# Inner form of one more fifth product, v asked for a unit sooner, and ScalarE's copies ahead of its sines, in a pooled-attention and snake-MLP kernel

## The chip, the cores and the metric

The kernel runs on one core of a Trainium2 chip. The metric is the device time of one execution in microseconds. The kernel before took 899.54 us (median of three runs, 898.81 to 899.56).

The engines are TensorE (PE; its weight loads are a row of their own, PEld), VectorE (DVE), ScalarE (ACT), GpSimd (POOL) and SyncE (SP), whose queue issues nearly all transfers here. Each engine runs its own instructions in program order and waits at an instruction whose inputs or whose place aren't ready.

## The reference

Everything is float32.

```python
def _attn_ref(q, k, v):              # each (8, 8, 576, 64)
    k_p = k.reshape(B, H, 72, 8, D).mean(axis=3)
    v_p = v.reshape(B, H, 72, 8, D).mean(axis=3)
    scores = np.matmul(q, k_p.transpose(0, 1, 3, 2)) / np.sqrt(D)
    attn = softmax(scores)           # over the 72 pooled keys
    return np.matmul(attn, v_p)

def _moe_ref(x, w_in, w_out, alpha): # x: (4608, 512), d_ff 2048
    h = x @ w_in
    s = np.sin(alpha * h)
    g = h + s * s / (alpha + 1e-09)
    return g @ w_out
```

The output of the attention, with heads side by side, is x.

## The kernel before, in words

**Stages.** The tokens go through the first matrix product in nine units of 512 tokens (units 0 to 8). While unit u is in TensorE, the attention of batch u+1 is worked out between its products. Units 1 to 6 are alike and last about 55 us each; the code calls them busy. Units 7 and 8 have no attention beside them. The second matrix product, `outputs`, fills the time from about 513 us on. The hidden values g go to DRAM (`g_bridge`) and come back.

**Seven products in place of eight.** Both matrix products are done by a scheme in which a 2x2 block product takes seven block products and some sums (`sums_of_x`, `combine_w_in`). In a unit there are four groups J = 0 to 3, each with seven slots k = 0 to 6. Slot number 7J + k is what the plan counts in, so group 1 has slots 7 to 13. In the slots the products come in the order 1, 5, 6, 2, 7, 3, 4. Each is four 128x128 by 128x256 matrix products, which the trace shows as eight records (an f32 product leaves two).

**Inner form.** `inner_product` works out one of these seven products by the same scheme once more, with blocks of 128 columns: seven small matrix products (fourteen records) in place of the eight records. It has four steps. Step a makes two of the small products in bank 7, and ScalarE copies them (L1062 into both halves of the result's bank, L1064 into a small tile m). Step b adds two products and ScalarE copies one quarter (L1068). Step d adds one product, and VectorE adds m (L1073). Step e adds the last two. The sums of weights come from `inner_w_in` once in unit 0, those of x from `inner_x` in slot 2 of each unit, both on GpSimd (L823). In busy units product 5 is done so in groups 2 and 3, and product 1 in group 3.

**Banks and the order within a group.** A group has four PSUM banks, b1, b6, b5, b7, drawn in turn from five, so b6, b5 and b7 of a group are b1, b6 and b5 of the group before, and its b1 is that group's spare, the b7 of the group before the last. Product 1 goes to b1; ScalarE copies it to b6 (L839), on which product 6 is added; b6 is copied to b7 (slot 3), and product 5's bank to an SBUF tile p5. Product 2 is added on b1, 7 on b7, 3 on b6 and 4 on b7. VectorE forms b7 + p5 in slot 5 and b6 + p5 in slot 6 (L838). Product 4 overwrites b7 after the first of these sums. ScalarE takes the sines (L1028) and squares (L1035); the last sines of a group are taken while the next group is in TensorE (`last_sines`, `squares`), and `finish` adds the squares on VectorE (L1080) before `store_g` sends the group off (L1094).

**Attention beside it.** `carry` writes the plan by hand: `at(slot, f)` puts a piece into a slot, where it is emitted at `extras()`. For units 1 to 6 it has the scores in slots 3 and 5 (L318) with their shifts on VectorE (L341, L342), then for four blocks i the exponentials on ScalarE (`exp`, L367), the reduction, reciprocal and scaling (`norm`, L373, L374 on VectorE, L375 on GpSimd) and the turning by VectorE (`turn`, L504 to L514). `move` sends the turned blocks to the tile aM, and `all_values` in slot 25 multiplies with v. Sines and exponentials have different tables on ScalarE: each change is an instruction of its own, ACT_TABLE_LOAD.

**v.** `load_v` issues six transfers (L141, L146) and has GpSimd add up the eight rows of each pool at once (`pool_rows`, L132). The smaller rest is added by `pool_v` in slot 12.

The plan for units 1 to 6, so far as the change touches it, is this:

```python
                at((8, 9, 10, 10)[i], A.exp, i)
                at((9, 10, 11, 12)[i], A.norm, i)
                at((12, 13, 13, 13)[i], A.turn, i)
            at(14, A.move, range(4))
            at(6, self.load_v, b)
            at(12, lambda: self.pool_v())
```

Of the kernel before, what the change touches and what calls it, by code (L numbers as in the profile page):

```python
# [19 lines left out]
P = 128  # L20
POOL = 8
TH = 256
JW = 2
# [17 lines left out]
class Kernel:  # L41
# [92 lines left out]
    def load_v(self, b):  # L134
# [12 lines left out]

        self.pool_rows(t, vm[:])

# [685 lines left out]
    def hidden(self, u, extra):  # L835
# [5 lines left out]
        busy = 0 < u < self.B - 1  # L841
        I5, I1 = ((2, 3), (3,)) if busy else {7: ((2, 3), (2, 3)), 8: ((2, 3), (2, 3))}.get(u, ((), ()))
        split = lambda J: u == 0 and J == 2
        end = lambda J: u == 0 and J == 3

# [31 lines left out]
        for slot in range(7 * self.NJ):  # L877
# [9 lines left out]
            if k == 0:  # L887
# [16 lines left out]
            elif k == 1:  # L904
                if not G.i1:
                    copy(G.b6[:], G.b1[:])
                if G.i5 and not G.i1:
                    self.last_sines(Q, 0)
# [8 lines left out]
            elif k == 2:  # L917
                if Q and not G.i5 and not split(J):
                    self.finish(Q)
                if not G.i1:  # L920
                    extras()
                if G.i1:
                    product(G, 6, G.b6, part=(0, 1))
# [15 lines left out]
            elif k == 3:  # L939
                late = J == 0 and busy  # L940
                if Q and not late and not G.i5 and not split(J):
                    self.store_g(Q)
# [10 lines left out]
                else:  # L953
                    copy(G.b7[:], G.b6[:])
                    if G.i5:
                        squares(Q, 1)
                        G.i5.d()
                        self.finish(Q)
                        self.store_g(Q)
                    else:  # L960
                        copy(G.p5[:], G.b5[:])
# [3 lines left out]
                    extras()  # L965
                    product(G, 2, G.b1)
            elif k == 4:
# [3 lines left out]
                else:  # L971
                    sin(G, 0, 0, G.b1)
                if not G.i5:
                    square(G, 0, 0)
# [4 lines left out]
                product(G, 7, G.b7, part=(0, 1))  # L979
                if G.i5:  # L980
                    if not G.i1:
# [41 lines left out]

    def sin(self, G, i, j, src):

        for jj in range(JW):
            f = i * self.K2 // 2 + G.J * JW + jj
            self.nc.scalar.activation(out=G.s[:, i, jj, j, :], in_=src[:, jj], func=AF.Sin, scale=self.al[:, f:f + 1])  # L1028
# [173 lines left out]
    def carry(self, u):  # L1202
# [6 lines left out]
        if u == 0:  # L1209
# [16 lines left out]
            at(7, self.load_v, 1)  # L1226
            at(7, lambda: self.pool_v())
            for i in range(2):
# [20 lines left out]
            at(9, self.load_q, 2)  # L1249
            at(23, lambda: self.inner_w_in(((5, 2, 4), (1, 3, 4)), (lambda w: [w[:, i * 2 * P:i * 2 * P + 2 * P] for i in range(8)])(self.q_tile(0))))  # L1250
            for e in range(2):
# [7 lines left out]
        if 0 < u < last:  # L1259
# [453 lines left out]
```

## Time and profile before

| | |
|---|---|
| median of three timed runs | 899.54 us |
| profiled execution, first to last instruction | 896.2 us |
| TensorE busy | 890.8 us, 99% |
| VectorE busy | 682.9 us, 76% |
| ScalarE busy | 438.6 us, 49% |
| GpSimd busy | 249.2 us, 28% |
| granted TensorE clock | 1.000 |
| length of a busy unit | 55.1 us (slot 25 at 129.9, 184.9, 240.0, 295.2 us) |

The page gives no other time of the profiled execution than its span; the timed runs include what lies around it. A line of the timeline gives the start, how long the instruction or the run of like instructions took, engine, line of the code, operation, the tiles written and read with their shapes, how many, and in brackets the idle time before it and what ended that. A line of the waits gives who waited for whom, the total in us, how often, and the longest. Records of TensorE overlap: the distance of two starts is the price of an instruction, and the length that is written is more than that. ScalarE's and VectorE's instructions overlap by about 0.1 us in the same way.

### The profile page before, as it was taken

The page shows a single profiled execution, that of the slowest core. Times are in us where ns is not written, and L with a number is a line of the kernel's source. Part 1 is how long each engine was busy: PE and PEld are TensorE (multiplying, and loading weights), DVE is VectorE, ACT ScalarE, POOL GpSimd, SP SyncE. Part 2 cuts the span into 40 slices and gives each one's busy share as a digit, 9 for nine tenths or more (in the row PEclk, how much of TensorE's full clock was granted, in tenths as well). Part 3 has the DMA queues.
Part 4 walks back from the last instruction along what each step waited for, and adds up shares of the span by engine and source line. Part 5 has one row for each costly group of instructions (what it writes and reads, how often), then busy time and mean ns, then how long its engine had stood idle before and what let it go on. Part 6 is the DMA issues. An engine that isn't in the chain of part 4 may idle for free.

```text
span 896.2 us, 16276 instructions
## 1 busy us (share of the span) xinstructions
PE 890.8 (99%) x6274; PEld 813.9 (91%) x6274; DVE 682.9 (76%) x918; ACT 438.6 (49%) x1033; POOL 249.2 (28%) x265
## 2 busy tenths in 40 slices
PE   9999999999999999999999999999999999999998
PEld 6787888888888888888888999999999999999998
DVE  7786857768577675765677889898897896996885
ACT  6687776877768777687776711111111211111111
POOL 6798443825338252434523000000000000000000
PEclk9999999999999999999999999999999999999999
DMA  9857957759586585648126243716435355164002
GB/s 269 244 158 206 244 147 212 187 164 254 139 214 186 183 225 147 175 140 302 53 106 219 102 181 103 232 37 218 117 105 160 89 159 159 37 192 142 20 18 53
DMA packets 119533, 141.03 MB, mean 157 GB/s; under 512 B 45776, under 2 KB 86496, under 8 KB 119456
## 3 DMA queue, kind: packets, MB, share of 16 engines
q1 hardware_dynamic: 116288, 137.39, 52.6%
q10 hardware_dynamic: 3168, 2.61, 1.0%
q8 instruction: 50, 0.82, 0.4%
q14 instruction: 27, 0.22, 0.1%
HBM read 75.37 MB, written 47.19 MB: 137 GB/s over the span
## 4 chain that ended last, share of the span: by engine, by line
PE 99%; DVE 0%; POOL 0%; ACT 0%; issue 0%; DVEq 0%
PE PS L866 44%; PE PS L1383 43%; PE PS L1058 5%; PE PS L318 2%; PE PS L613 2%; PE PS L626 1%; PE PS L1126 0%; PE PS L571 0%; PE PS L290 0%; PE PS L425 0%; PE PS L279 0%; PE PS L479 0%; PE PS L569 0%; POOL tr L451 0%; PE PS L403 0%; PE PS L487 0%
## 5 line engine op out<-in xcount | busy, mean ns | idle before, releaser
L866 PE MATMUL PS<-home,a 128*128 128x256 f32 x1072 | 253.0, 381 | 0.1
L866 PEld LDWEIGHTS PS<-home,a 128*128 128x128 f32 x1072 | 198.4, 190 | 30.9 <-issue 4.6
L866 PE MATMUL PS<-home,as 128*128 128x256 f32 x736 | 177.2, 382 | 0.0
L866 PEld LDWEIGHTS PS<-home,as 128*128 128x128 f32 x736 | 134.5, 190 | 18.1 <-ACT PS L839 1.2
L1383 PE MATMUL PS<-s,wb 128*128 128x192 f32 x672 | 116.2, 326 | 0.0
L1035 ACT ACTIVATE s<-s,c 128x256 f32<-128x256 f32 (+1 forms) x236 | 115.5, 556 | 0.0
L1383 PEld LDWEIGHTS PS<-s,wb 128*128 128x128 f32 x672 | 110.4, 190 | 0.1
L132 POOL TENSOR_TENSOR kvin<-kvin 96x768 f32<-96x768 f32 (+3 forms) x42 | 73.4, 1747 | 69.9 <-DMA kvin<-in_v_dram 67.8
L838 DVE TENSOR_TENSOR h<-PS,p 128x512 f32<-128x512 f32 x72 | 49.2, 684 | 55.5 <-PE PS L866 35.2
L1554 ACT COPY PS<-PS 128x192 f32<-128x192 f32 x42 | 12.7, 303 | 146.2 <-PE PS L1383 130.0
L1028 ACT ACTIVATE s<-h,al 128x256 f32<-128x256 f32 x144 | 65.5, 509 | 32.6 <-DVE h L838 32.6
L1383 PE MATMUL PS<-r,wb 128*128 128x192 f32 x432 | 79.0, 326 | 0.0
L1383 PEld LDWEIGHTS PS<-r,wb 128*128 128x128 f32 x432 | 71.6, 190 | 0.0
L1383 PE MATMUL PS<-s,a 128*128 128x192 f32 x384 | 70.2, 326 | 0.0
L1028 ACT ACTIVATE s<-PS,al 128x256 f32<-128x256 f32 x144 | 60.0, 469 | 17.2 <-PE PS L866 16.5
L1383 PEld LDWEIGHTS PS<-s,a 128*128 128x128 f32 x384 | 63.7, 190 | 0.0
L1080 DVE TENSOR_TENSOR h<-PS,s 128x512 f32<-128x512 f32 x36 | 24.8, 689 | 48.6 <-ACT s L1035 48.6
L839 ACT COPY PS<-PS 128x512 f32<-128x512 f32 x72 | 41.5, 577 | 34.5 <-PE PS L866 26.7
L1080 DVE TENSOR_TENSOR h<-h,s 128x1024 f32<-128x1024 f32 x36 | 55.3, 1537 | 3.3 <-ACT s L1035 3.1
L1584 ACT COPY PS<-PS 128x192 f32<-128x192 f32 x42 | 12.7, 303 | 89.5 <-PE PS L1383 89.5
L1322 DVE TENSOR_TENSOR s<-r 128x768 f32<-128x768 f32 x54 | 51.4, 951 | 4.8 <-PE PS L1383 2.8
L1383 PE MATMUL PS<-s,we 128*128 128x192 f32 x288 | 52.7, 326 | 0.0
(244 smaller groups left out, 1401.4 us busy)
## 6 DMA issues: line engine op xcount, KB each, us to landing
g_bridge<-h SPq DMA_DIRECT2D x72, 512.0 KB
r<-g_bridge SPq DMA_DIRECT2D x15, 1536.0 KB
x<-g_bridge SPq DMA_DIRECT2D x8, 1536.0 KB
out_dram<-o SPq DMA_DIRECT2D x90, 96.0 KB
kvin<-in_k_dram SPq DMA_DIRECT2D x14, 576.0 KB
q<-in_q_dram SPq DMA_DIRECT2D x7, 1024.0 KB
kvin<-in_v_dram SPq DMA_DIRECT2D x14, 512.0 KB
aM<-tr SPq DMA_DIRECT2D x54, 92.0 KB
```

The lines of the kernel that those rows point to most:

```text
L132: self.nc.gpsimd.tensor_tensor(out=t[..., 0:w] if w > D else out, in0=t[..., 0:w], in1=t[..., w:2 * w], op=OP.add)
L318: nc.tensor.matmul(ps[e][r0 + r:r0 + r + q.shape[-1], h, :], q[s], kb[s, hp, :], start=True, stop=True)
L613: nc.tensor.matmul(o[r:r + 64], w, x, start=start and i < 2, stop=False, skip_group_check=True)
L838: add = lambda o, x, y: nc.vector.tensor_tensor(out=o, in0=x, in1=y, op=OP.add)
L839: copy = lambda o, x: nc.scalar.copy(out=o, in_=x)
L866: nc.tensor.matmul(ps[:, jj, :], self.A[p][:, kk, f * P:(f + 1) * P], x[:, kk, :], start=(start and n == 0), stop=(kk == 1), skip_group_ch ...
L1028: self.nc.scalar.activation(out=G.s[:, i, jj, j, :], in_=src[:, jj], func=AF.Sin, scale=self.al[:, f:f + 1])
L1035: self.nc.scalar.activation(out=x, in_=x, func=AF.Square, scale=self.c[:, f:f + 1])
L1058: nc.tensor.matmul(o, W[m][:, G.J - J0], X[m], start=start and n == 0, stop=True, skip_group_check=True)
L1080: add = lambda o, x, y: self.nc.vector.tensor_tensor(out=o, in0=x, in1=y, op=OP.add)
L1322: tt = lambda o, x, y, op: nc.vector.tensor_tensor(out=o, in0=x, in1=y, op=op)
L1383: nc.tensor.matmul(out, W[:, J // 2, J % 2, :], A[:, J, :], start=(start and J == 0), stop=(J == self.NJ - 1), skip_group_check=True)
```

## The change

Five things change, all in units 1 to 6 but for a small one in unit 0.

- Product 5 of group 1 takes the inner form too. The sums of the weights for it are made over three groups in place of two, in the same tile of q, which is laid out anew.
- Group 1 has an order of its own (`fast`): half of product 4 of group 0 and its last sines come in slots 7 and 8 between the steps of the inner product; product 6 and product 2 are split in halves around steps d and e; p5 is copied after slot 10's exponentials. The second sines of group 1 are taken in slot 15, behind group 2's copies, in place of slot 13.
- The exponentials of blocks 0 and 1 go from slots 8 and 9 to slot 6, their norms from 9 and 10 to 7, the third norm from 11 to 10. Block 0 is turned in slot 9 in place of 12. A sine of one element (`sine_table`) behind the first two exponentials brings the table of sines back.
- v of batch b+1 is asked for in slot 21 of the unit before it is used in. Unit 1 still asks for its own in slot 6 too.
- GpSimd's adding of v (`pool_v_main`) is parted from the transfers: slot 6 in unit 1, slot 5 in units 2 to 6. In unit 0 both stay in slot 7.

```diff
-        self.pool_rows(t, vm[:])
+        self.pool_v_main = lambda: self.pool_rows(t, vm[:])
...
-        I5, I1 = ((2, 3), (3,)) if busy else ...
+        I5, I1 = ((1, 2, 3), (3,)) if busy else ...
+        fast = lambda G: busy and G.J == 1
...
             if k == 0:
                 if G.i5 and not N:
                     G.i5.a()
+                if fast(G):
+                    sin(Q, 0, 1, Q.g[:, 0, :, 1], (0,))
...
                     product(G, 1, G.b1, True)
-                    if G.i5:
+                    if G.i5 and not fast(G):
                         product(Q, 4, Q.b7, part=(2, 3))
             elif k == 1:
                 if not G.i1:
                     copy(G.b6[:], G.b1[:])
-                if G.i5 and not G.i1:
+                if fast(G):
+                    sin(Q, 0, 1, Q.g[:, 0, :, 1], (1,))
+                    G.i5.b()
+                    square(Q, 0, 1)
+                    product(Q, 4, Q.b7, part=(2, 3))
+                    self.last_sines(Q, 1)
+                    squares(Q, 1)
+                elif G.i5 and not G.i1:
+                    if fast(Q):
+                        sin(Q, 1, 1, Q.g[:, 1, :, 1])
                     self.last_sines(Q, 0)
...
             elif k == 2:
+                if fast(G):
+                    product(G, 6, G.b6, part=(0, 1))
+                    G.i5.d()
+                    self.finish(Q)
                 if not G.i1:
                     extras()
-                if G.i1:
+                if fast(G):
+                    product(G, 6, G.b6, part=(2, 3))
+                elif G.i1:
...
             elif k == 3:
                     copy(G.b7[:], G.b6[:])
-                    if G.i5:
+                    if fast(G):
+                        product(G, 2, G.b1, part=(0, 1))
+                        G.i5.e()
+                    elif G.i5:
...
                     extras()
-                    product(G, 2, G.b1)
+                    if fast(G):
+                        copy(G.p5[:], G.b5[:])
+                    product(G, 2, G.b1, part=(2, 3) if fast(G) else range(4))
...
             else:                      # k == 6
-                sin(G, 1, 1, G.g[:, 1, :, 1])
+                if not fast(G):
+                    sin(G, 1, 1, G.g[:, 1, :, 1])
...
+    def sine_table(self):
+        self.nc.scalar.activation(out=self.sm.tile([P, 1], F32, name="order")[:], in_=self.al[:, 0:1], func=AF.Sin)
...
             for i in range(4):
-                at((8, 9, 10, 10)[i], A.exp, i)
-                at((9, 10, 11, 12)[i], A.norm, i)
-                at((12, 13, 13, 13)[i], A.turn, i)
+                at((6,6,10,10)[i], A.exp, i)
+                at((7,7,10,12)[i], A.norm, i)
+            for i in range(4):
+                at((9,13,13,13)[i], A.turn, i)
+            at(6, self.sine_table)
             at(14, A.move, range(4))
-            at(6, self.load_v, b)
+            if u == 1:
+                at(6, self.load_v, b)
+            at(6 if u == 1 else 5, lambda: self.pool_v_main())
+            if b < last:
+                at(21, self.load_v, b + 1)
```

More of the change, by code (lines that the diff above doesn't have):

```diff
@@ L841, in hidden @@
         busy = 0 < u < self.B - 1
-        I5, I1 = ((2, 3), (3,)) if busy else {7: ((2, 3), (2, 3)), 8: ((2, 3), (2, 3))}.get(u, ((), ()))
+        I5, I1 = ((1, 2, 3), (3,)) if busy else {7: ((2, 3), (2, 3)), 8: ((2, 3), (2, 3))}.get(u, ((), ()))
         split = lambda J: u == 0 and J == 2
+        fast = lambda G: busy and G.J == 1
         end = lambda J: u == 0 and J == 3
@@ L940, in hidden @@
                 late = J == 0 and busy
-                if Q and not late and not G.i5 and not split(J):
+                if Q and not late and (not G.i5 or fast(G)) and not split(J):
                     self.store_g(Q)
@@ L972, in hidden @@
                     sin(G, 0, 0, G.b1)
-                if not G.i5:
+                if not G.i5 or fast(G):
                     square(G, 0, 0)
@@ L979, in hidden @@
                 product(G, 7, G.b7, part=(0, 1))
-                if G.i5:
+                if G.i5 and not fast(G):
                     if not G.i1:
@@ L1022, in hidden, with sin @@
                     product(G, 4, G.b7, part=(3,))
-    def sin(self, G, i, j, src):
-        for jj in range(JW):
+    def sin(self, G, i, j, src, cols=range(JW)):
+        for jj in cols:
             f = i * self.K2 // 2 + G.J * JW + jj
@@ L1226, in carry @@
             at(7, self.load_v, 1)
[L1227 removed]
+            at(7, lambda: (self.pool_v_main(), self.pool_v()))
             for i in range(2):
@@ L1249, in carry @@
             at(9, self.load_q, 2)
-            at(23, lambda: self.inner_w_in(((5, 2, 4), (1, 3, 4)), (lambda w: [w[:, i * 2 * P:i * 2 * P + 2 * P] for i in range(8)])(self.q_tile(0))))
+            at(23, lambda: self.inner_w_in(((5, 1, 4), (1, 3, 4)), (lambda w: [w[:, i * 3 * P:i * 3 * P + 3 * P] for i in range(4)] + [w[:, 12 * P + i * P:13 * P + i * P] for i in range(4)])(self.q_tile(0))))
             for e in range(2):
```

## The prediction

> **What bounds the kernel now.** I read the busy shares and the chain that ended last first, then TensorE's waits, then the timelines of one unit engine by engine, and last the stretch of unit 1 where GpSimd waits for v.
>
> ```profile
> PE 890.8 (99%) x6274; PEld 813.9 (91%) x6274; DVE 682.9 (76%) x918; ACT 438.6 (49%) x1033; POOL 249.2 (28%) x265
> PE 99%; DVE 0%; POOL 0%; ACT 0%; issue 0%; DVEq 0%
> PE PS L1126 <- DVE full L1597: 1.1, 1, 1.1
> PE PS L213 <- DMA h<-in_v_dram: 0.3, 1, 0.3
> ```
>
> TensorE is the bound and has no idle time in units 1 to 6 that could be taken away: its two waits lie in the first 12 us. So a gain can only come from less TensorE work, and a loss from a wait that does not exist today. Unit 3 (about 193.9 to 248.9) shows the prices. Its slot 5 begins at 205.59; slots 6 to 13, the second group's included, follow with no gap.
>
> ```profile
> 207.42 3.62 PE L866 MATMUL PS<-home,a 128*128 128x256 f32 x16
> 210.87 3.62 PE L866 MATMUL PS<-home,as 128*128 128x256 f32 x16
> ...
> 220.41 0.39 PE L1058 MATMUL PS<-home,as 128*128 128x128 f32 x2
> 220.63 0.39 PE L1058 MATMUL PS<-last,q 128*128 128x128 f32 x2
> 220.86 2.75 PE L866 MATMUL PS<-home,a 128*128 128x256 f32 x12
> ```
>
> The starts count, not the busy times: 16 wide records take 3.45 us (a plain product is 8 records, 1.725 us), 4 inner ones 0.45 us. ScalarE in the same stretch:
>
> ```profile
> 205.02 0.91 ACT L1028 ACTIVATE s<-h,al 128x256 f32<-128x256 f32 x2 [0.88 <-DVE h L838]
> 208.34 0.91 ACT L1028 ACTIVATE s<-h,al 128x256 f32<-128x256 f32 x2 [2.42 <-DVE h L838]
> ...
> 212.90 1.28 ACT L367 ACT_TABLE_LOAD   x1
> 214.20 1.26 ACT L367 ACTIVATE ex<-ex 128x576 f32<-128x576 f32 x2
> ...
> 217.86 1.28 ACT L1028 ACT_TABLE_LOAD   x1
> 219.16 0.84 ACT L1028 ACTIVATE s<-PS,al 128x256 f32<-128x256 f32 x2
> ```
>
> There is a hole of 2.42 us before 208.34, then work without a break until 222.05. Unit 1 lies 110.13 us earlier (sines at 109.03 against 219.16). There GpSimd and VectorE do this:
>
> ```profile
> 101.81 4.58 POOL L132 TENSOR_TENSOR kvin<-kvin 128x1024 f32<-128x1024 f32 x2 [11.26 <-DMA kvin<-in_v_dram]
> 106.46 0.73 POOL L132 TENSOR_TENSOR vm<-kvin 128x256 f32<-128x256 f32 x1
> 107.15 3.36 POOL L375 TENSOR_TENSOR ex<-ex,sm 128x576 f32<-128x576 f32 x3
> ...
> 107.89 0.69 DVE L838 TENSOR_TENSOR h<-PS,p 128x512 f32<-128x512 f32 x1
> 108.50 0.70 DVE L504 STREAM_TRANSPOSE tr<-ex 128x512 f32<-128x512 f32 x1
> ```
>
> GpSimd stands 11.26 us until v lands, adds it up until 107.19, and only then scales the softmax blocks (1.15 us each). Today VectorE turns block 0 after the sum of L838 that frees bank b7, so nobody on the path minds.
>
> **The change, part by part.**
>
> *The inner fifth product in group 1, units 1 to 6.* Eight records (1.725 us) become fourteen. Group 2 of unit 3 prices them from start to start: step a 0.45 (220.41), b 0.44 (224.38), d 0.22 (225.69), e 0.44 (228.50), together 1.55. TensorE saves 0.175 us a unit, 1.05 us in six. This lies wholly on the path. TensorE's new times in unit 3: slot 6, now only half a product, from 207.42; step a 208.28; slot 7's product 208.73 to 210.46; step b; halves of products 4 and 6 to 212.64; step d; half of 6 to 213.72; half of 2, step e, half of 2 to 215.9; slots 11 and 12 to 219.36; slot 13 from there.
>
> *ScalarE.* New per unit: two more table loads (2 x 1.28, from the rows above), three copies (0.30 + 0.20 + 0.16 start to start, L1062, L1064, L1068), and a one-element sine (about 0.1, by the one-element copy of L620). The order, with steps from unit 3's rows: the sines end 205.92; load 1.29, exponentials of blocks 0 and 1 1.27, load 1.29, one-element sine, so the step-a copy runs 209.9 to 210.27. TensorE wants it at 210.46: it fits by 0.19, all out of the hole. Then the m copy 0.2, a sine 0.41, the b6 copy (ends 211.4; wanted 211.77), a sine 0.41, the step-b copy (ends 211.95; wanted 212.64), squares 0.8, sines 0.72, wide squares 1.23, the b7 copy (ends 215.2; wanted 215.9), load 1.3, exponentials of blocks 2 and 3 1.4, the p5 copy (ends 218.47), load 1.3, sines from 219.78. Before, p5 was copied at 215.88 to 216.45, so this is 2.0 later.
>
> *What waits for p5.* VectorE's sum b7 + p5 starts at 218.5 and ends 219.2; slot 13 overwrites b7 at 219.36. Today that sum ends at 218.72 against 219.55. It still fits, by about 0.1 us after the 0.06 to 0.1 that a handover takes (a copy ending 223.36 let TensorE start at 223.45). In front of it on VectorE lie the closing sums of group 0 (now 214.73 to 216.6, behind the wide squares), the turn of block 0 (0.89, to 217.45) and the third norm's reduction (to 218.4, from 0.76 and 0.20): all in time in unit 3. I cost this at 0.02 us a unit, 0.1 in five; the bounds are 0 and 0.4 a unit, the latter if the chain of 13.9 us on ScalarE runs 3 per cent slower. I take the low end because its steps are rows of the same stretch, in the same neighbourhood.
>
> *Sines moved behind the next group's copies.* The sines of L1028 at 220.68 (0.80) go behind; the step-a copy of group 2 comes at about 221.3 instead of 221.48, its b6 copy still ends 0.1 before TensorE's product 6, as now. Cost 0. Cover: the moved sines' result is first read by the sums at 228.65.
>
> *v a unit sooner.* SP issues its six transfers (4.2 us, 202.24 to 206.46 now) after the group-1 store that ends at 236.67, so until 240.9; the turned q starts at 241.05 either way. The blocks aM are issued before. GpSimd adds v from 200.8 to about 206, in its idle 10.57 us, so the scaling comes at 212, on time. The q load comes up to 1 us sooner, the k load 1.8 later (behind the store of group 0); k is needed at 245.39. Cost 0 in units 2 to 6.
>
> *Unit 0 and A-sums.* Four sums over 384 instead of 256 columns: 0.28 more each by L823's 0.73 and 0.45, so GpSimd ends at 82.2 instead of 81.08, before 84.74 where it next waits for VectorE. Cost 0.
>
> *Unit 1.* Here v is still asked for in slot 6, GpSimd's adding still stands before the scaling, but the turn of block 0 is moved from slot 12 to slot 9, ahead of the sum b7 + p5 on VectorE. Block 0 is scaled at 108.30 (107.15 + 1.15). Then on VectorE: turn 0.82, the third norm 0.79 + 0.17, the sum 0.69, handovers 0.15: TensorE can begin slot 13 at 110.9, and wants to at 219.36 - 110.13 = 109.23. That is a new wait of up to 1.7. If GpSimd's second add took 1.28 as in unit 5 (323.26), not the 2.13 that it takes here beside VectorE's long sum, block 0 would be ready at 107.4 and the wait 0.8. In the new order that long sum runs from 105.2, against GpSimd's third add, so I stay near the upper end: 1.6. Behind it group 2 moves along with TensorE.
>
> **Sum.** -1.05 + 1.6 + 0.1 = +0.65 us on a span of 896.15, so 896.8. The page has no other time of that execution; the three timed runs' median, 899.54, is 3.4 above the span, which I add unchanged: 900.2.
>
> **A rule that speaks against it.** After each table load in unit 3 the next instruction starts 0.01 us later (12.90 + 1.28, then 14.20), and the load itself begins within 0.02 of its forerunner's end: a switch costs 1.3 in all. The Trainium skill, "ScalarE: Activation LUTs", section "What ACT_TABLE_LOAD costs", says that each switch costs a drain of about 1.38 us beside the load's 1.28. By the Trainium skill's page two more switches would be 5.3 us on ScalarE, not 2.6; the trace bears out the load and not the drain.
>
> **Rivals.** (1) *The gain alone.* Unit 1's wait doesn't come, because v lands earlier or the turn is not late. For it: the adds alone could end 0.9 sooner. Against it: GpSimd waits on the transfer itself and nothing before it in unit 1 is lighter. 899.54 - 1.05 = 898.5. (2) *Slower: ScalarE becomes the bound in slots 6 to 13.* It has no hole left between 205.9 and 221. If p5 comes 0.5 late, slot 13 waits 0.44 in units 2 to 6: +2.2, so 902.4. It decides from 0.23 us a unit, that is p5 0.3 late: (1.8 - 0.65)/5. For it: slacks of 0.1 to 0.2 at step b and at slot 13. Against: four places must hold and all do, by rows. (3) *A switch costs more than its load when ScalarE has no hole before it.* If each of the two extra switches around the first exponentials and the one before p5 cost as much again as its load, 1.28, step b would come 2.4 late and slot 13 1.2 more: 3.6 in each of six units, 22 in all, 921. No row shows such idle time behind a load. With the drain of the Trainium skill's page in place of that 1.28 it would be about 924.
>
> **How the numbers follow.** 0.2 per cent, 1.8 us, is about what a measurement of this kernel can tell from no change. Chances: my forecast 0.50, the gain alone 0.18, ScalarE bound 0.22, drain 0.02, something else 0.08. Within 0.2 per cent (897.74 to 901.34): 0.46 of mine, 0.15 of the first rival, 0.05 of the second, 0.04 of the rest, so 0.70. Slower: 0.04 + 0.17 + 0.02 + 0.03 = 0.26. Faster: 0.03 + 0.01 = 0.04, as the whole gain is 0.12 per cent. The range goes from just below the gain alone, 898.3, to the second rival with its price, 902.6; mine alone is 899.3 to 901.0 (unit 1 from 0.8 to 1.7, the small waits from 0 to 0.8).
>
> **What would show it.** Inner records of line 1058's code 14 per group 1 and a unit shorter by 0.17; a wait of TensorE in unit 1 near 109 to 111, released by VectorE, and none in the other units; four table loads a unit. It is wrong if TensorE waits in slot 8 or 13 of every unit, or if unit 1 shows none.

## The result, and the profile after

The changed kernel takes 903.35 us (median of five runs, 902.78 to 905.88) against 899.54 us before (five runs, 898.81 to 900.50). The ratio is 1.0051, with a 95% interval of 1.0039 to 1.0063: slower by half a per cent, 3.8 us by the medians (the ratio itself gives 4.6). The prediction was 900.2 us, at most 902.6, with "no change that can be measured" as the likeliest outcome; the time is above its range. Every line of code behind the new functions has another number now: ScalarE's copy after step a is L1089 (it was L1062), the inner products L1085 (L1058), VectorE's closing sums L1107 (L1080), the store L1121 (L1094).

The page of the changed kernel, its busy times and the chain that ended last by engine:

```profile
PE 890.4 (99%) x6310; PEld 813.6 (90%) x6310; DVE 680.6 (75%) x924; ACT 458.7 (51%) x1069; POOL 245.8 (27%) x265
PE 80%; SPq 7%; DMA 6%; ACT 3%; issue 1%; DVE 1%; POOL 1%; DVEq 0%; POOLq 0%
```

TensorE has as much work as before within 0.4 us, and ScalarE has 20 us more. What is new is in the second line: SP's queue and transfers hold 13% of the chain, where TensorE alone held 99%. TensorE's waits (who waits for whom: total us, times, longest) say where this meets it:

```profile
PE PS L1085 <- ACT PS L1089: 3.4, 4, 1.2
PE PS L213 <- DMA h<-in_v_dram: 1.4, 1, 1.4
PE PS L867 <- DVE h L838: 1.3, 1, 1.3
PE PS L1153 <- DVE full L1630: 1.1, 1, 1.1
```

The last line is the old wait at the start. The second is the start-up's wait for the first v, which lies at 12 us, ahead of every edit: it was 0.3 in the profiled execution before, and in those of the eleven other kernels below it is 0.6 to 1.3 seven times and not listed four times, so I don't count it to the change. The third is the wait in unit 1 that the prediction had priced. The first one is new: four times TensorE stands at step b of the inner product in group 1 until ScalarE has copied step a out of bank 7. These are units 3 to 6. Unit 3, TensorE:

```profile
205.97 1.53 PE L318 MATMUL PS<-kblk,q 64*64 64x72 f32 x80
...
210.34 0.39 PE L1085 MATMUL PS<-last,q 128*128 128x128 f32 x2
210.57 1.89 PE L867 MATMUL PS<-home,a 128*128 128x256 f32 x8
213.62 0.46 PE L1085 MATMUL PS<-last,q 128*128 128x128 f32 x2 [1.16 <-ACT PS L1089]
```

The product from 210.57 is eight records, 1.73 us from start to start, so step b was due at 212.30 and begins 1.32 late. By the same distance of starts units 4 to 6 lose 0.69, 0.96 and 1.13 (at 269.42, 325.31 and 381.37): 4.10 us in all. Unit 2 loses nothing.

ScalarE in the same stretch:

```profile
208.21 0.91 ACT L1052 ACTIVATE s<-h,al 128x256 f32<-128x256 f32 x2 [2.23 <-DVE h L838]
209.14 1.28 ACT L367 ACT_TABLE_LOAD   x1
210.43 1.26 ACT L367 ACTIVATE ex<-ex 128x576 f32<-128x576 f32 x2
211.71 1.28 ACT L1062 ACT_TABLE_LOAD   x1
213.00 0.20 ACT L1062 ACTIVATE order<-al 128x1 f32<-128x1 f32 x1
213.11 0.37 ACT L1089 COPY PS<-PS 128x256 f32<-128x256 f32 x1
```

The chain from the pair of sines to the copy is as predicted, without a gap: load 1.29, exponentials 1.28, load 1.29, one-element sine 0.11. It only begins too late, at 208.21, because the sines waited 2.23 us for VectorE's sum of slot 5. And that sum waited for a transfer. VectorE:

```profile
207.49 0.69 DVE L838 TENSOR_TENSOR h<-PS,p 128x512 f32<-128x512 f32 x1 [2.06 <-DMA g_bridge<-h]
```

Before, the same sum waited for TensorE alone, and only 0.71 us:

```profile
204.29 0.69 DVE L838 TENSOR_TENSOR h<-PS,p 128x512 f32<-128x512 f32 x1 [0.71 <-PE PS L866]
```

It writes into an h tile that the store of an earlier group still reads: it may not start until that store has landed. Measured from the start of slot 5's scores, the sum is on time at 0.16 us (before, and after in unit 2). In units 3 to 6 of after it comes 1.36, 0.72, 0.99 and 1.16 later than that, and TensorE's four waits are each 0.03 or 0.04 less: the lateness goes through ScalarE to step b almost whole. (The profile names the store for units 3, 5 and 6; in unit 4 it names TensorE's scores, which the sum doesn't read.) SP's queue shows why the store is late. First after, then before (unit 3 of each; unit 3 of after lies 1.84 us later, by the scores of slot 5, 205.97 against 204.13):

```profile
182.11 1.06 SPq L1121 DMA_DIRECT2D g_bridge<-h  x2
183.27 2.14 SPq L141 DMA_DIRECT2D kvin<-in_v_dram  x2
185.46 2.76 SPq L146 DMA_DIRECT2D vr<-in_v_dram  x4
188.31 12.70 SPq L244 DMA_DIRECT2D q<-tr  x16
201.11 4.24 SPq L1121 DMA_DIRECT2D g_bridge<-h  x4
```

```profile
179.88 1.06 SPq L1094 DMA_DIRECT2D g_bridge<-h  x2
185.99 10.64 SPq L244 DMA_DIRECT2D q<-tr  x16
196.73 5.42 SPq L1094 DMA_DIRECT2D g_bridge<-h  x4
202.24 1.44 SPq L141 DMA_DIRECT2D kvin<-in_v_dram  x2
```

Before, SP stood idle between the store of group 1 and the sixteen transfers of the turned q. After, v's six transfers fill that idle time, and the turned q starts nearly when it did (188.31 less 1.84 is 186.47, against 185.99). But its sixteen transfers now take 12.70 us, not 10.64. SP's own waits of units 2 to 6 put that down to v:

```profile
SPq L244 <- DMA kvin<-in_v_dram: 8.4, 5, 2.1
```

Before, in the same stretch, the turned q waits for VectorE's turning alone, and for nothing of v:

```profile
SPq L244 <- DVE tr L234: 18.7, 4, 5.1
```

Behind the turned q, on the same queue, stands the store of group 2 (the first two of the four at 201.11). It is issued 4.9 us ahead of slot 5's scores; before, it was 7.4 us ahead. These 2.5 us are 0.5 of later start and 2.1 of longer issue. In unit 2 the sum is on time although the store has no greater lead there, 4.7 us (146.37 against 151.07): it landed within 4.9 us of its issue, where the one of unit 3 took 6.4 by the end of VectorE's wait. Why it did isn't shown. That lead of 4.7 hangs on the wait of unit 1, as e2 below shows.

So the account of TensorE is: shorter work, 0.17 us a unit, which is -1.0 (by a later run without waits: a unit is 54.895 us from slot 25 to slot 25, against 55.065); unit 1's wait +1.45; the four waits at step b +4.10. This gives +4.5, where the medians differ by 3.8 and the ratio gives 4.6. The two spans differ by 901.6 - 896.2 = 5.4; with the 1.1 of the start-up wait the account gives 5.6.

### The profile page after: what moved, and what is told of

Read it like the earlier page. It is cut to its first block, busy times and chain, and to the rows that moved or that the text cites. A ratio compares the mean times of both kernels' runs of the same rounds, so it can differ in the third digit from the quotient of the medians.

```text
span 901.6 us, 16414 instructions
## 1 busy us (share of the span) xinstructions
PE 890.4 (99%) x6310; PEld 813.6 (90%) x6310; DVE 680.6 (75%) x924; ACT 458.7 (51%) x1069; POOL 245.8 (27%) x265
## 4 chain that ended last, share of the span: by engine, by line
PE 80%; SPq 7%; DMA 6%; ACT 3%; issue 1%; DVE 1%; POOL 1%; DVEq 0%; POOLq 0%
PE PS L1416 42%; PE PS L867 30%; PE PS L1085 4%; SPq L524 3%; DMA vr<-in_v_dram 3%; SPq L244 2%; DMA g_bridge<-h 2%; PE PS L613 1%; DMA kvin<-in_v_dram 1%; PE PS L318 1%; DMA h<-in_v_dram 1%; SPq L141 1%; SPq L1121 1%; ACT s L1052 1%; ACT L367 1%
## 5 line engine op out<-in xcount | busy, mean ns | idle before, releaser
L867 PE MATMUL PS<-home,a 128*128 128x256 f32 x1072 | 255.8, 381 | 1.4 <-DVE h L838 1.3
L867 PE MATMUL PS<-home,as 128*128 128x256 f32 x688 | 167.8, 382 | 0.0
L867 PEld LDWEIGHTS PS<-home,as 128*128 128x128 f32 x688 | 124.9, 190 | 16.5 <-ACT PS L839 1.2
L132 POOL TENSOR_TENSOR kvin<-kvin 96x768 f32<-96x768 f32 (+3 forms) x42 | 70.0, 1667 | 19.6 <-DMA kvin<-in_v_dram 17.6
L1107 DVE TENSOR_TENSOR h<-PS,s 128x512 f32<-128x512 f32 x36 | 24.8, 690 | 44.1 <-ACT s L1059 44.1
L375 POOL TENSOR_TENSOR ex<-ex,sm 128x576 f32<-128x576 f32 (+1 forms) x28 | 35.3, 1272 | 66.4 <-DVE sm L374 45.4
```

Of the source, the lines that this page charges most:

```text
L132: self.nc.gpsimd.tensor_tensor(out=t[..., 0:w] if w > D else out, in0=t[..., 0:w], in1=t[..., w:2 * w], op=OP.add)
L375: nc.gpsimd.tensor_tensor(out=E(i), in0=E(i), in1=sm.unsqueeze(2).to_broadcast([P, n, Sp]), op=OP.mult)
L867: nc.tensor.matmul(ps[:, jj, :], self.A[p][:, kk, f * P:(f + 1) * P], x[:, kk, :], start=(start and n == 0), stop=(kk == 1), skip_group_ch ...
L1107: add = lambda o, x, y: self.nc.vector.tensor_tensor(out=o, in0=x, in1=y, op=OP.add)
```

## The experiments

The theory after the result: **the late store**. v's place on SP's queue, ahead of the turned q, makes the store of group 2 late; its landing frees the h tile; VectorE's sum and ScalarE's sines go late, and since the change filled ScalarE's hole with two table loads, the lateness reaches TensorE's step b. The rivals: **ScalarE alone** (the chain of slot 6 is too long whatever SP does), and **transfers in flight** (v's bytes slow the store, wherever it is issued).

**v behind the store, kernel e1.** v is asked for in slot 26, behind the store of group 2 in SP's queue.

```diff
-                at(21, self.load_v, b + 1)
+                at(26, self.load_v, b + 1)
```

> Edit: v of the next batch is asked for in slot 26, so that SP issues it behind the store of group 2, in place of slot 21, ahead of the turned q and that store. Theory A (late store): the waits of TensorE at step b of group 1 in units 3 to 6 (1.32, 0.69, 0.96, 1.13 us, 4.1 together) come from the store of group 2 of the unit before, which SP now issues 2 to 3 us later behind v; its landing frees the h tile that VectorE's sum of slot 5 writes, and behind that sum stand the sines, the table load, the exponentials and the step-a copy. So these four waits go, unit 1's wait of 1.45 stays: 903.35 - 4.1 = about 899.2. Rival B (ScalarE is the bound by itself): its chain from slot 6 is too long whatever the store does, so 903.3. Rival C (bytes): v's 1.25 MB slow the store on the transfer engines, whatever the order of issue; here v comes after the store, so 899.2 as by A.

Measured: 904.55 us, ratio 1.0057 (1.0041 to 1.0073). The waits at step b are gone in all units, and VectorE's sum waits for no transfer: in this the theory held. The time did not come back, because something else came in. Beside unit 1's wait, which is still there, TensorE's waits now have this line:

```profile
PE PS L318 <- issue: 4.6, 2, 2.4
```

and TensorE in unit 3:

```profile
206.45 1.52 PE L318 MATMUL PS<-kblk,q 64*64 64x72 f32 x79
210.37 0.22 PE L318 MATMUL PS<-kblk,q 64*64 64x72 f32 x1 [2.40 <-issue]
```

79 of the 80 scores of slot 5 run, then TensorE stops for 2.4 us at the last one and waits for nothing that the profile shows; in unit 5 the same happens 27 scores before the end (322.35, 2.22). What the transfers were doing from 197 to 207.5 us, by queue (packets, MB, share of 16 engines), and then from 207.5 to 212.5:

```profile
q1 hardware_dynamic: 1276, 2.37, 86.5%
```

```profile
q1 hardware_dynamic: 767, 1.36, 77.1%
q8 instruction: 2, 0.03, 3.2%
```

v, the stores of groups 2 and 3 and the turned q follow one another without a pause. In ten microseconds no packet of the instruction queue q8 is served; the first comes at 207.62 and the second at 211.50. Before, one came at 200.74. So the stop looks like TensorE's own code arriving late. In both stops, and in the two of e3 below, TensorE goes on 2.5 to 2.8 us after such a packet starts (319.73 and 322.35 in unit 5). This is a reading, not yet a test; g1 below bears on it.

**Block 0 of unit 1 turned late, kernel e2.** VectorE's order in unit 1 is put back as it was.

```diff
-                at((9,13,13,13)[i], A.turn, i)
+                at((12 if u == 1 else 9,13,13,13)[i], A.turn, i)
```

> Edit: in unit 1 alone block 0 is turned in slot 12, as before the change, in place of slot 9. If unit 1's wait of 1.45 us at slot 13 comes from the turn that stands in front of the sum b7 + p5 on VectorE and waits for GpSimd's scaling behind the adding of v, it goes: 903.35 - 1.45 = 901.9, and the waits of units 3 to 6 stay. Rival: the sum waits for p5, which ScalarE copies 2 us later than before, and a wait of some tenths up to the whole stays: 902 to 903.3.

Measured: 904.06 us, 1.0052 (1.0039 to 1.0065). The wait in unit 1 is gone, as expected, and nothing is won that the timed runs can tell:

```profile
PE PS L1085 <- ACT PS L1089: 3.0, 5, 0.9
```

There are five waits at step b now in place of four. Unit 2, which had none, loses 0.77, and the others 0.79, 0.72, 0.44 and 1.04. The wait in unit 1 had given unit 2's store its time: without it the store's lead on slot 5's scores is 3.5 us (147.29 against 150.81) in place of 4.7, and its lateness is paid from unit 2 on. In the profiled executions the waits of units 1 to 6 add up to 3.76 us here and 5.55 in the changed kernel.

**Both, kernel e3.** e1 and e2 together.

```diff
-                at((9,13,13,13)[i], A.turn, i)
+                at((12 if u == 1 else 9,13,13,13)[i], A.turn, i)
...
-                at(21, self.load_v, b + 1)
+                at(26, self.load_v, b + 1)
```

> Both edits: v behind the store of group 2 and the late turn in unit 1. Theory A with the turn theory: no new wait of TensorE is left and the gain of the inner form alone remains, 903.35 - 4.1 - 1.45 = 897.8, about 1.0 to 1.7 below the kernel before. Rival B: 901.9. If v so late makes GpSimd's adding late in its turn (block 0 scaled after slot 9 of units 2 to 6), new waits at slot 13 of those units, each up to 1: 898 to 902.

Measured: 904.45 us, 1.0056 (1.0036 to 1.0076). No wait at step b and none in unit 1, but TensorE's waits for nothing shown are there again, in units 3 and 5, 2.40 and 2.50 us. Something else comes behind them in this profiled execution, the slowest of the six: for 3.41 us from 209.81, and again from 322.45, the granted clock is 0.50 where it is 1.00 otherwise. Eight records that take 1.83 us in f1 take 2.83 there, and the two stretches cost 3.3 us by the starts. In e1 the granted clock stays at 1.00 behind the same two stops. The mean granted clock of the other runs of e1 and e3 is 0.997 to 1.000, and the fastest of each (902.26 and 901.06 us) has 1.000, so part of the spread of these two kernels may be this.

So the two repairs add up in what they remove, and the stops that come with v in slot 26 eat it. This miss left the theory of the late store likely but not shown by time.

**The store on another queue, kernel e4.** All else as in the changed kernel; v and the turned q stay where they are on SP. Only the store of group 2 in units 1 to 5 is issued by GpSimd.

```diff
-            self.nc.sync.dma_start(out=self.gd[...
+            (self.nc.gpsimd if Q.J == 2 and 0 < Q.u < self.B - 2 else self.nc.sync).dma_start(out=self.gd[...
```

> Edit: only the store of group 2 of units 1 to 5 is issued by GpSimd, so it doesn't stand behind v and the turned q in SP's queue; v stays in slot 21. Theory A (order of issue on SP): the store is issued 4 to 6 us sooner and the four waits at step b go: about 899.2. Rival C (bytes of v and of the turned q in flight): the store lands late all the same, waits stay at least in part: 901 to 903.3. Rival B: 903.3.

Measured: 899.27 us, 0.9998 (0.9989 to 1.0007), as expected. No unit waits at step b; what is left in units 1 to 6 is unit 1's wait, 1.03 us by the starts. The store leaves at 189.77, 11.3 us earlier than in the changed kernel, and VectorE's sum of slot 5 waits only for TensorE again:

```profile
189.77 1.47 POOL L1121 DMA_DIRECT2D g_bridge<-h  x2 [9.75 <-DVE h L1107]
```

```profile
206.70 0.69 DVE L838 TENSOR_TENSOR h<-PS,p 128x512 f32<-128x512 f32 x1 [0.71 <-PE PS L867]
```

v and the turned q go out from 183.83 to 201.49, as late as in the changed kernel. The store's two transfers take 7.7 and 9.0 us to land among them, but they have the time. So it is the store's place in the queue; h1 below tests this without a second queue, and the rival "transfers in flight" falls with it. Against the changed kernel's 1.0051 this one line is worth some 4 to 5 us.

**The store on GpSimd and the turn late, kernel f1.** e4 and e2 together.

```diff
-            self.nc.sync.dma_start(out=self.gd[...
+            (self.nc.gpsimd if Q.J == 2 and 0 < Q.u < self.B - 2 else self.nc.sync).dma_start(out=self.gd[...
...
-                at((9,13,13,13)[i], A.turn, i)
+                at((12 if u == 1 else 9,13,13,13)[i], A.turn, i)
```

> Edit: the store of group 2 of units 1 to 5 issued by GpSimd, and in unit 1 block 0 turned in slot 12. In the run with that store alone TensorE's waits at step b were gone and one wait was left, 1.03 us at slot 13 of unit 1. Theory (order of issue on SP, and the early turn in unit 1): that wait goes too, 899.27 - 1.0 = 898.2, with no new wait of TensorE in units 1 to 6. Rival (the sum b7 + p5 waits for ScalarE's late p5 in any case): a wait of 0.2 to 1 stays in unit 1, 898.5 to 899.3.

Measured: 897.93 us (897.36 to 899.17), 0.9986 (0.9977 to 0.9995). TensorE waits for no other engine and no transfer in units 1 to 6; the list of its waits has only these two lines, neither of them in these units:

```profile
PE PS L1153 <- DVE full L1630: 1.1, 1, 1.1
PE PS L213 <- DMA h<-in_v_dram: 0.7, 1, 0.7
```

What is left is the gain of the inner product, which the prediction's first rival had put at 898.5. It has the lowest median of this study, and its interval lies below 1.

**Only the order on SP, kernel h1.** No other queue: the last eight of the sixteen transfers of the turned q are asked for one slot later, so that the store of group 2 stands in their midst; block 0 of unit 1 is turned late.

```diff
-                at((9,13,13,13)[i], A.turn, i)
+                at((12 if u == 1 else 9,13,13,13)[i], A.turn, i)
...
-                at(((turn, turn + 1) if u == 0 else (23, 24))[part] if part < 2 else turn + part, self.turn_q, u + 2, part)
+                at(((turn, turn + 1) if u == 0 else (23, 24))[part] if part < 2 else turn + part + (u > 0 and part == 3), self.turn_q, u + 2, part)
```

> The changed kernel with two edits, all transfers on SP as in the change: in units 1 to 6 the last eight turned-q transfers come in slot 26 in place of 25, so that SP issues the store of group 2 ahead of them, about 5 us sooner; and in unit 1 block 0 is turned in slot 12. v stays in slot 21. Theory A (order on SP's queue alone): the store is no later than before the change, VectorE's sum of slot 5 does not wait for it, the waits at step b go, and with the late turn no wait is left: about 898. Rival C (bytes in flight): the store still lands late behind v and half of the turned q, waits of 0.3 to 1.3 us stay: 900 to 903. If the late half of q comes too late for slot 5's scores, TensorE waits there.

Measured: 898.06 us, 0.9990 (0.9982 to 0.9999). SP in unit 3:

```profile
187.57 7.47 SPq L244 DMA_DIRECT2D q<-tr  x8
195.15 1.19 SPq L1121 DMA_DIRECT2D g_bridge<-h  x2
196.38 6.62 SPq L244 DMA_DIRECT2D q<-tr  x8
```

The store leaves at 195.15 in place of 201.11, and none of units 1 to 6 waits at step b or slot 13. One wait of 0.64 us is in unit 4, at the scores that read the half of q sent late: the price of what was put behind. (Another of 0.7 is in unit 0, ahead of the edits.) So the order on one queue, with the same queue and the same bytes, decides. (The late turn, this kernel's other edit, had left the waits at step b in place in e2.)

**v sooner without the rest, kernel f2.** The kernel before, with v's transfers and adding as in the change and nothing else of it.

```diff
...
-            at(6, self.load_v, b)
+            if u == 1:
+                at(6, self.load_v, b)
+            at(6 if u == 1 else 5, lambda: self.pool_v_main())
+            if b < last:
+                at(21, self.load_v, b + 1)
```

> The kernel before with only v moved: transfers in slot 21 of the unit before, GpSimd's adding in slot 5 (unit 1 as in the change), product 5 of group 1 plain, exponentials, norms and turns where they were. Theory A: the store of group 2 is just as late and VectorE's sum of slot 5 waits for it up to 2 us in units 3 to 6, but ScalarE's hole of 2.42 us and the plain group 1 cover it: TensorE has no new wait, 899.3, same. Rival: the late store costs TensorE time by itself, 900 to 903.

Measured: 899.77 us, 1.0006 (0.9997 to 1.0014): no change that can be told. VectorE waits for the late store here too (6.0 us, four times, against 5.6, three times, in the changed kernel), though it is spread otherwise: by the scores of slot 5 its sum is 0.2 to 0.7 us late in units 2 to 5 and 2.1 in unit 6, 3.8 in all against 4.2. ScalarE in unit 3:

```profile
208.02 0.91 ACT L1028 ACTIVATE s<-h,al 128x256 f32<-128x256 f32 x2 [1.38 <-DVE h L838]
210.85 0.91 ACT L1028 ACTIVATE s<-h,al 128x256 f32<-128x256 f32 x2 [1.92 <-DVE h L838]
```

The sines are late, and behind them is the hole (1.92 us are still left of the 2.42 in the prediction's lines), which swallows it. TensorE waits once, 0.61 us in unit 6, where the lateness is greatest. So v's new place costs nothing that can be told alone, and the filled hole costs nothing alone (f3, next). Together they cost 4 us.

**v in its own unit, kernel f3.** The changed kernel with v's transfers and adding back in slot 6 of the unit that uses it, and block 0 turned in slot 12 in all units.

```diff
-                at((9,13,13,13)[i], A.turn, i)
+                at((12,13,13,13)[i], A.turn, i)
...
-            if u == 1:
-                at(6, self.load_v, b)
-            at(6 if u == 1 else 5, lambda: self.pool_v_main())
-            if b < last:
-                at(21, self.load_v, b + 1)
+            at(6, self.load_v, b)
+            at(6, lambda: self.pool_v_main())
```

> The changed kernel with v as before the change (transfers and adding in slot 6 of its own unit) and, since the scaling then stands behind the adding, block 0 turned in slot 12 in all units. Inner form, early exponentials and ScalarE's order stay. Theory A: the store is on time, no wait at step b; the turn behind the sum b7 + p5, so no wait at slot 13 either: the gain of the inner form alone, 899.27 - 0.8 to 1.0 = about 898.4. Rival B (ScalarE's chain is too long by itself): step b waits in each unit, 900 or more.

Measured: 898.56 us, 0.9994 (0.9986 to 1.0003), as expected; one wait at step b, 0.33 us in unit 3. The inner product needs neither v sooner nor the early turn. (Its gain is too small to be told here: the interval holds 1.)

**Without the one-element sine, kernel f4.** One line fewer; the sines' table is then loaded by the next sine, behind the copies of step a.

```diff
-            at(6, self.sine_table)
```

> The changed kernel without the one-element sine behind the first exponentials, so the sines' table is loaded at the first sine of slot 7, behind the step-a copies. Theory (the wait moves along ScalarE's chain): the step-a copy comes 1.4 us sooner and step b no longer waits, but the b6 copy stands behind load and sine as before, and TensorE now waits for it at product 6, 0.4 less than at step b (its slack there is larger by that): waits of 0.3 to 0.9 in units 3 to 6, 902 to 903. Rival (it is the step-a copy alone that is late): all waits of units 3 to 6 go, 899 to 900.

Measured: 905.1 us, 1.0062 (1.0047 to 1.0078). The waits at step b are gone. They have moved to the next copy, b6, which product 6 is added on:

```profile
PE PS L867 <- ACT PS L839: 2.0, 4, 0.8
```

0.48, 0.96, 0.47 and 0.79 us in units 3 to 6 by the starts, with a further 0.18 at slot 13 in units 2 to 6, 0.73 in unit 1 and 0.64 in unit 4. Those at the b6 copy were expected, the others not, and the time is 2 us above what was. So in this stretch what is let through at one copy is charged at the next.

**A known delay on ScalarE, kernel f5.** f1, which has no waits, plus two squares of 128 columns behind the one-element sine, whose results nothing reads.

```diff
+        self.nc.scalar.activation(out=self.last[:, 512:640], in_=self.ident[:], func=AF.Square)
+        self.nc.scalar.activation(out=self.last[:, 512:640], in_=self.ident[:], func=AF.Square)
```

> The kernel with the store of group 2 by GpSimd and the late turn in unit 1 (897.93, no wait of TensorE in group 1), with two squares over 128 columns added on ScalarE behind the one-element sine of units 1 to 6, some 0.5 to 0.6 us of extra work ahead of the step-a copy. Their results are not used. My sum gave the step-a copy 0.19 us of slack; then step b waits 0.3 to 0.4 us in each of six units, 897.93 + 2.1 = 900.0, and little more is lost behind it. Rival (the slack is larger than 0.6, as the store's lateness of 1 to 2 us would need to explain waits of 0.4 to 1.3): 898.0.

Measured: 901.68 us, 1.0032 (1.0020 to 1.0045). ScalarE and then TensorE, unit 3:

```profile
211.78 0.29 ACT L1063 ACTIVATE last<-ident 128x128 f32<-128x128 f32 x1
212.10 0.31 ACT L1064 ACTIVATE last<-ident 128x128 f32<-128x128 f32 x1
212.32 0.37 ACT L1091 COPY PS<-PS 128x256 f32<-128x256 f32 x1
```

```profile
210.59 1.89 PE L867 MATMUL PS<-home,a 128*128 128x256 f32 x8
212.83 0.46 PE L1087 MATMUL PS<-last,q 128*128 128x128 f32 x2 [0.35 <-ACT PS L1091]
```

The copy is 0.54 us later, and step b, due at 212.32, comes 0.51 us late, in each of the six units (and 0.07 more on the record behind). Six times that is 3.5, and f5 stands 3.75 above f1. So the slack of this place is about 0.03 us, as by the late sums of the changed kernel, and not the 0.19 that I had expected the delay to meet. In f1 the copy ends at 210.84 and step b starts at 211.01, which looks like 0.17 us to spare; but where TensorE does wait for it, it starts 0.14 after the copy's end (212.69 to 212.83). The spare time was the handover.

**v's two large transfers later still, kernel g1.** As e1, but only the four small transfers of v are in slot 26; the two large ones go in slot 6 of the next unit, behind the store of group 3, with the adding there, and block 0 is turned in slot 12.

```diff
...
-                at((9,13,13,13)[i], A.turn, i)
+                at((12,13,13,13)[i], A.turn, i)
...
             if u == 1:
                 at(6, self.load_v, b)
-            at(6 if u == 1 else 5, lambda: self.pool_v_main())
+            else:
+                at(6, lambda: self.load_v_main())
+            at(6, lambda: self.pool_v_main())
             if b < last:
-                at(21, self.load_v, b + 1)
+                at(26, self.load_v, b + 1, True)
```

> The changed kernel with v's transfers behind the store of group 2 as in the earlier run, but only the four small ones in slot 26; the two large ones (1 MB) come in slot 6, behind the store of group 3, with GpSimd's adding behind them, and block 0 is turned in slot 12 in all units. In the earlier run TensorE stood 2.4 and 2.2 us in units 3 and 5 in the middle of slot 5's scores, waiting for nothing that the profile shows, while the transfer engines were full from 199.6 to 210 us and no packet of the instruction queues came for ten us before. Theory (TensorE's own code came late behind that traffic): with 1 MB less in front of slot 5 these two waits go, and no wait at step b or slot 13 is left: about 898.5. Rival (they come from the place of v's code in the queues or from the inner form): they stay, 903.

Measured: 903.97 us, 1.0063 (1.0049 to 1.0077). The two stops for nothing shown are gone, and q8's packets come ahead of the scores (207.45) in unit 3, at 204.24, and at 316.77 in unit 5. This speaks for the reading of e1, that full transfer engines kept TensorE's code away, but one 0.33 us wait at step b is back in unit 3. The time stayed high for another reason:

```profile
PE PS L871 <- ACT PS L843: 5.0, 5, 1.3
```

1.50, 1.10, 1.34, 1.22 and 0.67 us in units 2 to 6 in group 2, at the copy of b6. v lands later there, so GpSimd adds and scales later; that this is the chain which holds up VectorE and then ScalarE was read from the trace and not tested.

## Why the prediction was wrong, point by point

**"TensorE is the bound, a gain can only come from less TensorE work, and a loss from a wait that does not exist today."** Right. All of the loss lies in waits that were not there.

**The inner product, 0.175 us a unit.** Right: 0.17 us in f1.

**Unit 1, a new wait of 1.6 us.** Right, in place and cause: 1.45 us. TensorE, then GpSimd and VectorE, in unit 1 of the changed kernel:

```profile
108.15 1.89 PE L867 MATMUL PS<-home,as 128*128 128x256 f32 x8
111.33 1.13 PE L867 MATMUL PS<-home,a 128*128 128x256 f32 x4 [1.28 <-DVE h L838]
```

```profile
102.26 3.71 POOL L132 TENSOR_TENSOR kvin<-kvin 128x1024 f32<-128x1024 f32 x2 [11.08 <-DMA kvin<-in_v_dram]
106.05 1.63 POOL L132 TENSOR_TENSOR vm<-kvin 128x256 f32<-128x256 f32 x1
107.64 2.25 POOL L375 TENSOR_TENSOR ex<-ex,sm 128x576 f32<-128x576 f32 x2
```

```profile
105.88 1.22 DVE L1107 TENSOR_TENSOR h<-h,s 128x1024 f32<-128x1024 f32 x1
108.82 0.71 DVE L504 STREAM_TRANSPOSE tr<-ex 128x512 f32<-128x512 f32 x1 [1.73 <-POOL ex L375]
```

GpSimd stands until v lands, adds, and only then scales block 0; VectorE waits 1.73 us to turn it, and slot 13 waits for the sum behind the turn. e2, which undoes the early turn in unit 1 alone, removes the wait. The sum added it as independent, though, and by e2 it was not, since it sheltered unit 2. With the store on time it is: e4 waits 1.03 us here, and f1, without the wait, is 1.3 us faster.

**Table loads at 1.3 us, no drain.** Right. The loads at 209.14 and 211.71 are each followed within 0.01 us by the next instruction, with no hole before them on ScalarE now. By the Trainium skill, "ScalarE: Activation LUTs", section "What ACT_TABLE_LOAD costs", another 1.38 us of drain was to be reckoned with. No load here shows it, and f1 with all the new loads is faster than before.

**"v a unit sooner ... the turned q starts at 241.05 either way ... Cost 0 in units 2 to 6."** This is the step that failed. Its fact was nearly right: the turned q starts 0.5 us later in unit 3, since v's six transfers took 4.95 us on SP and not 4.2. The step ended there. It didn't ask how long the sixteen transfers would take with v ahead of them (12.70 us, not 10.64), nor what stood behind them on SP's queue (the store of group 2), nor what that store's landing frees (the h tile that VectorE's sum of slot 5 writes). It listed the loads of q and k behind v and not the store. The price is 4.10 us in units 3 to 6. With it the sum's +0.65 becomes the +4.5 of the account, for the terms of unit 1 and slot 13 were only 0.15 and 0.1 too high; so it is the whole of the error. e4 takes it away by moving the store and nothing else, h1 by moving half of q (and unit 1's turn). By its own signs the prediction asked for no wait outside unit 1; the waits are in slot 8, at step b.

**"It fits by 0.19, all out of the hole."** The number was right (0.17 in f1 from the copy's end to step b) and its meaning wrong: a handover, for which the prediction took off 0.06 to 0.1 at slot 13 and which is 0.14 by f5, was not taken off here. With a slack of 0.03 us every lateness ahead passes on to TensorE in full. The prediction knew that ScalarE's hole of 2.42 us was spent on table loads; it didn't ask what that hole had been covering, or would have to cover. f2 shows that: with the hole there, 3.8 us of lateness in all cost TensorE one wait of 0.61.

**Slot 13 in units 2 to 6, 0.1 of slack.** Held: no wait there in the changed kernel.

**3.4 us outside the span.** Wrong. In all five timed runs of the changed kernel about 1.8 us lie outside the span (903.35 and 901.6 in the profiled one). By that the profiled execution before took about 898.0 us, 1.6 below its timed median. The profiled execution was a lucky one, and comparing spans alone would have shown the loss larger than it is. The forecast is not moved by it, since the change was in effect added to the median.

**The rivals.** The second, ScalarE as the bound in slots 6 to 13, came nearest in time, 902.4, and named step b as one of two thin places. But it reckoned slot 13 to wait in five units because ScalarE's own chain ran long. The chain ran as costed; it started late. The third rival's times are not added on one base (on 900.2 its 3.6 us in six units give 921.8, not 921, and the larger figure gives 923.4, not 924), and nothing like them was measured. The upper bound of the small waits, too, is 2.0 in one place (0.4 in each of five units) and 0.8 in another. The first rival, 898.5, is near what f1, h1 and f3 gave with the store on time (897.93, 898.06, 898.56): the gain was real, by the intervals of f1 and h1, and it was paid back four times over by the place of a transfer.

## What to carry to other kernels

When transfers are moved ahead on a queue, follow everything that stays behind them on it to the end: how long it now takes, when it lands, which tile that frees, and who writes that tile next. A hole in an engine's timeline is spent only once, so before filling one, ask which lateness upstream it swallows now; afterwards an engine without a hole passes on each tenth of a microsecond, less only the slack that is left after the handover. And a wait that is removed may have sheltered a later one (e2, f4): price waits in a chain together.

## What the runs showed of the hardware that was not expected

- With SP's transfers back to back for some ten microseconds (share of the transfer engines 1.0), TensorE twice stopped for 2.4 and 2.2 us in the midst of a run of like instructions, waiting for nothing that the trace shows (e1; 2.4 and 2.5 in e3). The packet of the instruction queue came at 207.62, where by the scores of slot 5 (206.45 against 204.13 before, and 200.74 for the packet) it would have been due at 203.1. Where the packets came on time (g1), the stops were gone. That the code was late is the likeliest reading, and was not shown beyond this.
- Behind both stops of e3 the granted clock was 0.50 for 3.41 us, which cost 3.3 us in all; behind the stops of e1, as long, it stayed at 1.00.
- GpSimd's third add of v took 1.63 us in unit 1 in place of 0.73, beside VectorE's 1.22 us sum of two SBUF tiles from 105.88; the first two, no longer beside it, took 3.71 in place of 4.58. The sum moved, and with it which add was the slow one (in unit 5 of the kernel before it is likewise the third, 3.71 and 1.59).
- From the end of a ScalarE copy to the start of a TensorE product waiting for it: 0.14 us (f5).
- The start-up's wait for the first v differs by more than 1 us between executions of like kernels (0.3 to 1.4 where it is listed), as much as the whole gain of this change.

What stays open: why the profile's account of after (+4.5 us) fits the ratio and is 0.7 above the difference of the medians; why a store of group 2 landed sooner in unit 2 than in unit 3; and why e2 and f4 are 1.1 us slower in the median than in the execution that was profiled. In that execution f4's waits do account for its time: 6.1 us by the starts, with the 0.1 on the record behind each, where its span is 6.2 above f1's.
